# A gated recurrence with a feed-forward layer on one core: the second group's decay steps on VectorE, and all steps in a new order

## The chip, the cores and the metric

The kernel runs on one core of a Trainium2 chip. The metric is the time of one execution on the device in microseconds. Before the change it is 265.83 us, the median of five runs (265.01 to 266.19).

The engines are called as the profile calls them: PE (TensorE) for matmuls, DVE (VectorE) and POOL (GpSimd) for elementwise work, ACT (ScalarE) for functions such as Exp, Ln, Arctan, Sin and Tanh, SP (SyncE), which issues most of the DMAs. POOL issues some DMAs too.

## The reference

Inputs are q, k, v, a_re and a_im, each of shape (4 batches, 8 heads, 768 steps, 48 channels) in float32, and three weights, 384x1536, 384x1536 and 1536x384. A complex recurrence runs over the steps; its real part is read out with q, and the result, seen as 3072 tokens of 384, goes through a gated feed-forward layer.

```
mag = sqrt(a_re*a_re + a_im*a_im)
scale = minimum(mag, 0.999) / (mag + 1e-06)
ar, ai = a_re*scale, a_im*scale
for t in range(S):
    new_re = ar*S_re - ai*S_im          # (ar, ai at step t, along d)
    new_im = ar*S_im + ai*S_re
    S_re, S_im = new_re + outer(k[t], v[t]), new_im
    y[t] = q[t] @ S_re
x = y as (3072, 384)
out = (sigmoid(x @ w_gate) * (x @ w_val)) @ w_out
```

## The kernel before

**Slabs and groups.** The 768 steps are cut into 6 chunks of 128, so there are 24 slabs (chunk c, batch b), numbered m = 4c + b. Slabs are worked on in eight groups g of 2, 2, 4, 4, 4, 4, 2, 2 (SIZES, L34). Group 0 is slabs 0 and 1, group 1 is slabs 2 and 3, all of chunk 0; group 2 is chunk 1, and so on.

**The steps of a group, by the names that the kernel gives them.**
- lr, la: a_re and a_im of a slab into one tile `a` (L556, SP). sq: both squared (L583 on DVE for slabs 2 to 8, else L586 on ACT).
- add: the sum of the two squares (L592). min: the cap, min and max in one instruction for two slabs (L599). lnm: Ln of it (L613, ACT). cl: its sum over the steps of the chunk, a matmul with a triangle (L633). ee: Exp of half of it with both signs (L640, L642). scr, rbe, arr: the chunk's last row through DRAM into columns.
- lna, inv: Ln of a_re, and Exp of minus that, which is 1/a_re (L607, L618, ACT). r: the ratio a_im/a_re for two slabs (L624). atan: its arctangent (L702). hop: the angle at the end of the chunk before, added by a small DMA that POOL issues (L714). ct: the sum of angles over the steps (L722); r16 and nid take whole turns off (L728, L735). cr: the last angle for the next hop (L745). ab, cs: sine and cosine (L756, L767 to L770).
- lk, lq, lv: loads of k, q and v (L556, SP); v16: v as f16 (L688, POOL). qke: k and q times the two decay factors, one instruction for a slab (L695). ks, qs: times cosine and sine, to f16 (L780).
- tp, qkT: transposes on PE and their copy by DVE (L818, L819, L825), from slab 13 on DMA transposes instead. sc: scores (L837). mst: times the causal mask (L845). y: the read-out (L903 with the carried state, L905 with the scores). kv, u, x16, P: the state that is carried from chunk to chunk (L859, L868, L877, L887, L890).
- y16, xp, xt: y to f16, transposed, into the group's input of the feed-forward layer (L522, L923, L929). pg and pv: two times three matmuls for each of 12 blocks of 128 of the 1536 (L942). tanh: the gate on ACT (L952). p: gate times value on DVE (L958). po: the third matmul (L978). ot, st: result to SBUF (L522) and out (L996).

**Which engine.** add, min, r and qke are issued through a helper that takes the group number; with BRISK = 1 (L30) only group 0 has them on DVE:

```
def eng(g):
    return nc.vector if g < BRISK else nc.gpsimd
```

**What sets the order.** The order of all steps is written out by hand, as numbers: TIMES has one number for each step, and the steps are issued in the order of these numbers, each engine getting its instructions in that order and running them in it. A step's waits follow from the data. The numbers serve as sort keys only. Before a function of ACT that the loaded table doesn't have, a table load is put in (L1006).

```
order = sorted(self.steps, key=lambda k: (at[k], self.rank[k]))
```

SLOTS names, tile by tile in order of allocation, which of a kind's few buffers the tile gets (2 buffers for `a2`, `sq`, `lm`, `cs`, 5 for `qk`, 4 PSUM banks each for `gen` and `moe`, and so on). WARM names steps ahead of which PE multiplies a tile of zeros a number of times, into the tile that the step then overwrites (L1012); there are 465 such matmuls in all.

```
for _ in range(WARM.get(key, 0)):
    nc.tensor.matmul(warm_of(tiles[st[2][0]]), zero, zero, start=True, stop=True)
st[0](tiles)
```

The nine weight loads (wg, wv, wo, thirds of w_gate, w_val and w_out, L541 and L548) are issued by POOL between its other instructions, at places that TIMES sets too. The first six feed pg and pv: blocks 0 to 3 need the first third, 4 to 7 the second, 8 to 11 the last.

Of the kernel before, what the change touches and what calls it, by code (L numbers as in the profile page):

```python
# [29 lines left out]
BRISK = 1  # L30
# [6 lines left out]
        32.951, 14.583, 29.638],  # L37
    "wv": [
        41.185, 24.111, 37.481],
    "wo": [  # L40
        56.204, 51.226, 63.509],
    "lr": [
        0.04, 0.86, 3.16, 5.08, 13.925, 19.752, 28.021, 17.531, 29.623,
        62.128, 43.583, 64.048, 57.026, 74.047, 73.257, 65.008, 96.257,
        107.615, 110.045, 101.515, 137.663, 151.768, 166.927, 171.067],
    "la": [
        2.2, 0.45, 4.12, 7, 14.68, 15.64, 25.512, 24.552, 30.593, 69.119,
        51.877, 58.495, 61.138, 75.967, 72.847, 63.088, 97.077, 105.695,
        103.265, 102.675, 139.203, 141.828, 168.878, 168.468],
    "sq": [  # L50
        5.69, 4.73, 9.161, 10.49, 21.424, 23.242, 34.706, 33.84, 44.15,
        72.689, 57.636, 69.729, 66.044, 80.249, 76.577, 70.689, 104.472,
        112.973, 118.73, 115.322, 149.228, 158.967, 174.676, 175.97],
    "add": [
        6.559, 7.025, 10.178, 12.149, 22.441, 26.922, 36.527, 34.857, 53.807,
        73.594, 58.541, 70.634, 66.949, 89.758, 79.981, 72.602, 111.571,
        123.103, 119.884, 117.287, 150.133, 161.218, 175.581, 177.193],
    "min": [
        7.605, 13.68, 30.458, 38.521, 74.873, 71.699, 91.293, 87.116, 124.638,
        121.415, 162.282, 179.123],  # L60
    "lna": [
        6.558, 13.727, 35.687, 78.872, 83.739, 120.761, 160.998, 178.729],
    "lnm": [
        8.185, 15.332, 39.488, 82.363, 93.681, 125.605, 163.249, 180.206],
    "inv": [
        7.426, 14.595, 37.195, 80.986, 91.565, 126.982, 163.986, 180.943],
    "r": [
        8.295, 15.623, 42.005, 39.424, 82.531, 84.291, 93.956, 106.636,
        133.282, 137.885, 164.891, 181.848],
    "cl": [  # L70
        9.073, 9.719, 20.075, 17.308, 43.684, 45.402, 46.048, 42.48, 85.5,
        91.202, 87.197, 87.843, 109.442, 108.149, 111.386, 107.503, 148.529,
        150.473, 145.491, 154.559, 177.162, 179.303, 182.338, 182.984],
    "ee": [
        12.987, 12.247, 22.019, 22.759, 47.25, 48.311, 49.051, 46.51, 90.085,
        92.941, 89.345, 90.825, 111.417, 110.677, 112.233, 109.46, 152.06,
        151.32, 152.8, 155.406, 179.466, 188.022, 187.282, 188.762],
    "scr": [
        30.033, 30.313, 28.711, 28.431, 49.147, 48.867, 50.638, 56.303,
        91.661, 94.511, 90.731, 91.381, 115.548, 116.608, 114.858, 110.455,  # L80
        156.012, 152.178, 156.292, 156.982, 183.077, 198.269, 192.333, 192.613],
    "rbe": [
        47.412, 67.694, 70.599, 98.417, 129.307, 159.322, 213.64, 204.94],
    "lk": [
        9.88, 6.04, 7.96, 20.712, 35.106, 41.425, 53.205, 32.273, 78.847,
        81.727, 83.647, 77.887, 115.138, 96.667, 104.225, 133.664, 114.448,
        116.198, 156.572, 141.418, 176.447, 181.157, 169.288, 172.027],
    "lq": [
        11.8, 10.84, 22.632, 21.672, 38.894, 46.157, 55.893, 37.894, 79.807,
        92.351, 91.941, 82.687, 120.194, 101.105, 109.085, 134.074, 119.784,  # L90
        117.158, 157.262, 146.226, 177.407, 184.327, 178.947, 183.367],
    "lv": [
        23.592, 12.76, 50.228, 49.427, 8.92, 75.007, 80.767, 76.927, 92.761,
        84.607, 114.038, 111.965, 119.374, 136.703, 106.655, 128.527, 145.816,
        94.101, 111.005, 121.814, 191.923, 206.91, 205.76, 172.987],
    "v16": [
        31.509, 17.384, 57.244, 54.761, 13.104, 79.404, 86.539, 81.909,
        103.832, 104.408, 118.728, 120.839, 130.217, 145.197, 110.655,
        132.706, 169.908, 113.392, 127.88, 168.466, 198.411, 218.557, 220.232,
        183.609],  # L100
    "qke": [
        15.915, 14.389, 27.877, 25.162, 49.465, 52.046, 61.748, 47.704,
        95.717, 97.478, 99.239, 92.196, 128.457, 115.039, 135.043, 141.784,
        155.763, 152.242, 166.705, 157.524, 186.109, 196.651, 188.357, 193.916],
    "atan": [
        10.216, 19.618, 43.84, 86.41, 117.353, 147.043, 184.404, 190.796],
    "ct": [
        11.426, 13.076, 25.634, 21, 49.401, 50.047, 52.307, 54.263, 92.496,
        93.142, 95.408, 90.356, 130.362, 122.671, 135.255, 129.716, 155.205,
        163.471, 166.078, 164.117, 193.531, 197.936, 199.73, 198.917],  # L110
    "r16": [
        12.273, 13.923, 26.481, 25.575, 50.248, 50.894, 55.627, 62.519,
        93.343, 96.075, 99.028, 91.869, 133.139, 123.937, 138.869, 133.605,
        156.052, 164.944, 167.011, 169.332, 195.244, 199.482, 202.877, 203.943],
    "nid": [
        13.722, 14.523, 27.081, 26.727, 50.848, 51.817, 56.538, 64.118,
        95.245, 96.701, 104.303, 94.435, 135.093, 128.568, 141.444, 137.196,
        156.948, 165.748, 170.162, 171.619, 196.323, 200.376, 205.919, 214.499],
    "cr": [
        19.248, 20.355, 30.395, 30.765, 55.525, 55.895, 58.653, 66.781,  # L120
        97.782, 101.447, 107.796, 98.152, 137.227, 144.056, 144.426, 141.165,
        158.597, 170.192, 185.618, 173.352],
    "ab": [
        18.25, 15.449, 28.61, 27.546, 52.95, 52.484, 59.067, 64.782, 95.609],
    "cs": [
        18.25, 17.363, 28.61, 29.608, 52.95, 54.738, 59.067, 64.782, 100.183,
        99.026, 106.162, 103.315, 135.456, 129.652, 141.807, 139.532, 157.44,
        166.112, 170.562, 172.195, 196.687, 201.864, 206.282, 214.862],
    "ks": [
        19.692, 18.716, 29.74, 32.974, 54.147, 56.093, 63.916, 66.125,  # L130
        102.751, 101.019, 108.206, 110.129, 136.745, 130.941, 143.096,
        148.631, 159.249, 167.943, 175.372, 184.196, 200.213, 210.119,
        207.571, 216.165],
    "qs": [
        22.29, 20.558, 31.205, 37.37, 57.07, 59.923, 69.298, 68.432, 104.816,
        101.885, 109.263, 110.995, 140.302, 131.807, 145.477, 149.497,
        164.078, 170.962, 176.838, 185.062, 202.011, 215.299, 208.437, 222.773],
    "tp": [
        28.731, 23.29, 26.28, 21.645, 35.6, 35.154, 40.597, 38.934, 62.039,
        59.39, 67.868, 65.458, 81.249, 79.852, 77.107, 78.532, 112.679,  # L140
        117.708, 115.091, 104.466, 123.54, 114.644, 118.804, 116.388, 153.513,
        146.785],
    "qkT": [
        30.606, 24.977, 26.947, 28.012, 36.771, 39.279, 41.245, 39.878,
        62.985, 61.255, 71.71, 74.679, 82.056, 81.125, 77.755, 79.552,
        116.498, 118.355, 115.9, 107.008, 125.003, 115.301, 120.485, 117.097,
        154.826, 147.433],
    "sc": [
        34.93, 31.247, 28.504, 30.801, 37.762, 40.012, 47.846, 43.126, 76.333,
        76.557, 78.978, 75.783, 86.974, 84.274, 80.298, 82.023, 119.651,  # L150
        121.374, 116.834, 113.126, 125.91, 123.317, 125.687, 122.248, 157.111,
        156.075, 151.119, 152.639, 160.33, 155.851, 159.057, 158.834, 180.596,
        180.82, 189.87, 191.616, 191.84, 190.093, 194.8, 194.577, 219.4,
        214.661, 221.347, 220.274, 218.527, 226.605, 227.483, 227.707],
    "mst": [
        35.572, 32.375, 29.076, 36.172, 41.843, 40.476, 48.271, 43.55, 78.953,
        76.981, 80.151, 78.354, 87.398, 85.118, 83.72, 82.654, 121.084,
        122.149, 117.695, 114.102, 126.711, 124.403, 126.111, 123.338,
        157.717, 157.118, 151.561, 153.064, 161.349, 156.518, 160.75, 160.15,
        181.021, 181.62, 190.294, 192.041, 193.106, 190.894, 195.71, 196.309,  # L160
        220.361, 217.63, 222.173, 220.96, 219.761, 227.029, 227.908, 230.424],
    "kv": [
        56.338, 51.617, 68.314, 72.159, 91.002, 102.808, 115.538, 122.471,
        120.524, 138.006, 153.959, 132.303, 168.667, 157.334, 171.782,
        177.808, 201.834, 215.532, 216.379, 220.497],
    "P": [
        58.601, 52.018, 75.994, 73.548, 91.403, 113.636, 119.553, 122.872,
        121.683, 145.011, 154.36, 134.071, 173.896, 158.317, 173.43, 178.209,
        211.584, 218.829, 219.295, 223.639],
    "y": [  # L170
# [238 lines left out]
def kernel(  # L409
# [107 lines left out]
    def eng(g):  # L517
        return nc.vector if g < BRISK else nc.gpsimd

# [523 lines left out]
```

## Time and profile before

| | |
|---|---|
| median of five runs | 265.83 us (265.01 to 266.19) |
| the profiled execution | 265.22 us |
| its span, first to last instruction | 263.5 us |
| busy PE, DVE, ACT, POOL | 95%, 80%, 69%, 62% of the span |
| TensorE clock granted | 1.00 throughout |
| matmuls of zeros (L1012) | 465, 31.9 us busy |
| sums on POOL, L592 | 22, 1302 ns mean; on DVE 2, 554 ns |
| caps on POOL, L599 | 11, 889 ns mean; on DVE 1, 560 ns |
| ratios on POOL, L624 | 11, 1883 ns mean; on DVE 1, 950 ns |
| decay products on POOL, L695 | 22, 2054 ns mean; on DVE 2, 1791 ns |
| bytes moved | 38.18 MB, 145 GB/s mean |

The span begins with the first and ends with the last instruction; the execution's time has some 1.7 us more around it. A mean over a form is the time of one instruction from its start to its end; successive instructions of an engine overlap a little, so the distance of their starts is shorter than that (0.48 us between sums on DVE that take 0.55). On PE the overlap is larger: three matmuls of 128x512 are shown as 0.81 us and start 0.65 us after the three before them.

### The profile page before, as it was taken

The numbers are of one execution on the slowest core, as the hardware profiler recorded it, in microseconds if no ns is written. First come the engines' busy times: TensorE is split into PE (matmuls) and PEld (weight loads), VectorE is DVE, ScalarE is ACT, GpSimd is POOL, SyncE is SP. The second block draws the span as 40 slices with busy tenths as digits, with TensorE's granted clock in tenths as the row PEclk, the third lists the DMA queues.
The fourth block names the chain that finished last, engine by engine and source line by source line (L and its number), as shares of the span: only waits on it lengthen the run. The fifth ranks groups of instructions, "written<-read, shape, count | busy, mean of one in ns | idle before, by whom it ended". The sixth has DMA issues, their size and how long they took to land.

```text
span 263.5 us, 6444 instructions
## 1 busy us (share of the span) xinstructions
PE 250.4 (95%) x2445; PEld 172.9 (66%) x2445; DVE 211.6 (80%) x373; ACT 182.5 (69%) x304; POOL 163.3 (62%) x170
## 2 busy tenths in 40 slices
PE   8797898899899999999999999999999999999995
PEld 8576786668688854547764457754556644678784
DVE  2778798489989965999989888988668978986552
ACT  3999356975468999989586897889993665114250
POOL 1284889799069999759999969782879400420000
PEclk9999999999999999999999999999999999999999
DMA  7999999999988929999729998689986288641001
GB/s 142 214 163 197 191 186 201 154 171 197 175 98 161 217 52 194 156 201 201 146 63 165 208 149 147 92 198 175 200 159 73 91 151 140 63 119 63 30 32 60
DMA packets 175022, 38.18 MB, mean 145 GB/s; under 512 B 167928, under 2 KB 174992, under 8 KB 174992
## 3 DMA queue, kind: packets, MB, share of 16 engines
q1 hardware_dynamic: 170368, 34.20, 68.9%
q0 software_dynamic: 4624, 3.57, 9.8%
q8 instruction: 19, 0.31, 0.5%
q14 instruction: 11, 0.09, 0.1%
HBM read 30.74 MB, written 4.76 MB: 135 GB/s over the span
## 4 chain that ended last, share of the span: by engine, by line
PE 72%; SPq 9%; DVE 7%; ACT 6%; issue 3%; DMA 3%; DVEq 0%; ACTq 0%
PE o L978 18%; PE v L942 16%; PE g L942 15%; SPq L556 9%; PE cl L633 5%; PE ct L722 4%; PE sc L837 4%; PE y L905 2%; PE y L903 2%; PE tp L818 2%; PE tp L819 1%; DVE qst L780 1%; DMA a<-in_a_re_dram 1%; PE xp L923 1%; PE kv L877 1%
## 5 line engine op out<-in xcount | busy, mean ns | idle before, releaser
L952 ACT ACTIVATE g<-g 128x256 f16<-128x256 f32 (+1 forms) x96 | 44.6, 492 | 37.5 <-PE g L942 28.7
L958 DVE SCALAR_TENSOR_TENSOR p<-g,v 128x256 f16<-128x256 f16 (+1 forms) x96 | 50.5, 548 | 14.6 <-PE v L942 7.6
L942 PE MATMUL v<-xt,wv 128*128 128x256 f16 (+1 forms) x288 | 58.4, 326 | 1.3 <-DVE p L958 1.2
L942 PE MATMUL g<-xt,wg 128*128 128x256 f16 (+1 forms) x288 | 58.0, 325 | 0.4 <-DVE p L958 0.3
L978 PE MATMUL o<-wo,p 128*128 128x384 f16 (+1 forms) x300 | 55.6, 319 | 0.0
L592 POOL TENSOR_TENSOR lm<-sq 128x384 f32<-128x384 f32 x22 | 28.6, 1302 | 29.4 <-ACT sq L586 14.6
L695 POOL TENSOR_TENSOR qk<-qk,ee 128x768 f32<-128x768 f32 x22 | 43.6, 2054 | 1.1 <-DMA qk<-in_q_dram 0.8
L942 PEld LDWEIGHTS <-wv 128*128 128x128 f16 x288 | 27.3, 98 | 20.8 <-issue 3.4
L942 PEld LDWEIGHTS <-wg 128*128 128x128 f16 x288 | 27.4, 97 | 19.6 <-issue 3.2
L845 DVE TENSOR_TENSOR mst<-sc,msk_t 128x512 f16<-128x512 f32 x48 | 31.8, 683 | 7.5 <-PE sc L837 6.9
L978 PEld LDWEIGHTS <-p 128*128 128x128 f16 x300 | 27.1, 98 | 13.0 <-issue 0.2
L1006 ACT ACT_TABLE_LOAD x27 | 34.6, 1283 | 0.5
L1012 PEld LDWEIGHTS <-zero 128*128 128x128 f16 x465 | 29.9, 103 | 6.5 <-issue 4.6
L780 DVE TENSOR_TENSOR kst<-qk,cs 128x768 f16<-128x768 f32 x24 | 25.0, 1043 | 2.3 <-ACT cs L770 1.3
L780 DVE TENSOR_TENSOR qst<-qk,cs 128x768 f16<-128x768 f32 x24 | 25.3, 1059 | 0.0
L624 POOL TENSOR_TENSOR a<-a 128x768 f32<-128x768 f32 x11 | 20.7, 1883 | 2.7 <-ACT a L618 2.3
L633 PE MATMUL cl<-lm,wl_t 128*128 128x384 f32 x48 | 19.6, 504 | 2.7 <-ACT lm L613 2.0
L714 POOL DMA_DIRECT2D a<-cr x20 | 16.9, 1030 | 5.9 <-ACT a L702 5.5
L688 POOL TENSOR_SCALAR v<-v 128x384 f16<-128x384 f32 x24 | 16.2, 675 | 5.7 <-DMA v<-in_v_dram 2.9
L722 PE MATMUL ct<-a,wt_t 128*128 128x384 f32 x48 | 19.6, 503 | 0.1
L825 DVE COPY qkT<-tp 128x1024 f16<-128x1024 f16 x26 | 17.4, 682 | 1.3 <-PE tp L819 1.1
L768 ACT ACTIVATE cs<-ct 128x384 f32<-128x384 f32 x24 | 11.8, 491 | 9.4 <-DVE cs L756 9.4
(71 smaller groups left out, 441.2 us busy)
## 6 DMA issues: line engine op xcount, KB each, us to landing
a<-in_a_re_dram SPq DMA_DIRECT2D x24, 192.0 KB
a<-in_a_im_dram SPq DMA_DIRECT2D x24, 192.0 KB
qk<-in_k_dram SPq DMA_DIRECT2D x24, 192.0 KB
v<-in_v_dram SPq DMA_DIRECT2D x24, 192.0 KB
qk<-in_q_dram SPq DMA_DIRECT2D x24, 192.0 KB
out_dram<-ot SPq DMA_DIRECT2D x23, 192.0 KB
wg<-in_moe_w_gate_dram POOLq DMA_DIRECT2D x3, 384.0 KB, 6.0
wv<-in_moe_w_val_dram POOLq DMA_DIRECT2D x3, 384.0 KB, 5.9
```

The lines of the kernel that those rows point to most:

```text
L592: eng(g).tensor_tensor(out=T[LM][:, s], in0=T[SQ][:, 0], in1=T[SQ][:, 1], op=ALU.add)
L633: nc.tensor.matmul(T[CL][:, :HD], wl_t, T[LM][:, s], start=True, stop=True)
L695: eng(g).tensor_tensor(out=T[QK], in0=T[QK], in1=T[EE], op=ALU.mult)
L722: nc.tensor.matmul(T[CT][:, :HD], wt_t, T[A][:, 1, s], start=True, stop=False, skip_group_check=True)
L780: nc.vector.tensor_tensor(out=T[SL][i].rearrange("p h (r x) -> p h r x", r=2)[:, :, :, 0:D], in0=heads(T[QK][:, i]).unsqueeze(2) .broadcas ...
L845: nc.vector.tensor_tensor(out=T[MS], in0=T[SC], in1=msk_t.unsqueeze(1).broadcast_to([L, 4, L]), op=ALU.mult)
L942: nc.tensor.matmul(T[ACC][:, :nt], w[:, j, fb * 128:fb * 128 + 128], T[XT][:, j, :nt], start=(j == 0), stop=(j == 2))
L952: nc.scalar.activation(out=T[G16][:, :nt], in_=T[PG][:, :nt], func=FT.Tanh, scale=0.5)
L958: nc.vector.scalar_tensor_tensor(out=T[PT][:, fb, :nt], in0=T[G16][:, :nt], scalar=1.0, op0=ALU.add, in1=T[PV][:, :nt], op1=ALU.mult)
L978: nc.tensor.matmul(T[PO][:, :wd], T[PT][:, fb, s * L:(s + 1) * L], wo16[:, fb, c0:c0 + wd], start=(fb == 0), stop=(fb == NFB - 1))
L1006: nc.scalar.preload_act_table_set(SETS[key[1]])
L1012: nc.tensor.matmul(warm_of(tiles[st[2][0]]), zero, zero, start=True, stop=True)
```

## The change

BRISK goes from 1 to 2, so that add, min, r and qke of group 1 are issued on DVE. These are two sums (128x384), one cap, one ratio and two decay products (128x768 each). TIMES, SLOTS and WARM have new numbers throughout: every kind of step has other sort keys, most tiles another buffer, and there are 411 matmuls of zeros in other places. No function is changed.

```
-BRISK = 1
+BRISK = 2
...
     "wg": [
-        32.951, 14.583, 29.638],
+        37.288, 33.328, 40.992],
     "wv": [
-        41.185, 24.111, 37.481],
+        14.906, 24.802, 28.527],
...
     "min": [
-        7.605, 13.68, 30.458, 38.521, 74.873, 71.699, 91.293, 87.116, 124.638,
-        121.415, 162.282, 179.123],
+        7.605, 12.962, 27.624, 38.328, 80.098, 69.74, 90.34, 81.001, 123.736,
+        125.795, 162.811, 178.675],
...
     "qke": [
-        15.915, 14.389, 27.877, 25.162, 49.465, 52.046, 61.748, 47.704,
...
+        18.035, 17.169, 29.555, 25.694, 49.066, 51.647, 62.667, 53.408,
...
     "ct": [
-        11.426, 13.076, 25.634, 21, 49.401, 50.047, 52.307, 54.263, 92.496,
...
+        11.649, 13.132, 19.238, 23.515, 49.004, 51.593, 52.239, 53.926,
...
     "hop": [
-        45.384, 45.964, 46.544, 47.124, 88.598, 89.178, 90.713, 88.018, 127.3,
...
+        45.249, 46.049, 47.583, 48.163, 89.76, 88.6, 89.18, 88.02, 128.08,
...
 WARM = {
-    ('cl', 0): 86,
-    ('ct', 0): 19,
-    ('ct', 1): 18,
-    ('sc', 0, 0): 62,
-    ('sc', 0, 1): 4,
-    ('sc', 1, 0): 15,
-    ('sc', 1, 1): 18,
...
-    ('cl', 2): 38,
-    ('cl', 3): 47,
-    ('ct', 2): 34,
-    ('ct', 3): 5,
...
+    ('cl', 0): 78,
+    ('ct', 0): 23,
+    ('ct', 1): 15,
+    ('sc', 0, 0): 21,
+    ('sc', 0, 1): 8,
+    ('sc', 1, 0): 71,
...
+    ('cl', 2): 16,
+    ('cl', 3): 69,
+    ('ct', 3): 19,
+    ('sc', 2, 0): 23,
...
```

How the front of each engine's order changes, as far as it is spoken of below:
- DVE, between the ratio of group 0 and the last square of group 2. Before: sq of slabs 2 and 3, r16 of 0 and 1, qke, ab, qke, ab, ks, ks, qs, sq, qs, sq, a qkT copy, r16 of 3 and 2, and so on. After: sq, add, sq, add of group 1, r16 of slab 0, min, r16 of slab 1, ab, r of group 1, two qke of group 0, ab, ks, ks, qs, qs, sq, r16 of 2 and 3, sq, qke of slab 3, ab, two qkT copies, ab, sq, qke of slab 2, a copy, ks, qs, a mask, ks, sq.
- ACT, after its second table load. Before: four Exp of group 0 (ee), lna, inv, lnm of group 1, table, cs, cs, cr, atan. After: lna, four Exp, lnm, inv, table, cs of slab 1, atan, cs of slab 0.
- POOL. Before, it begins with the two sums of group 1. After: cast of v, first third of w_val, cast of v, a sum of group 2 and so on; the last two sums of group 2 are followed by the first third of w_gate, the cap, a ratio, the last third of w_gate, a ratio, two hops, a sum of group 3, two hops.
- PE: the first of pg and pv is preceded by seven cl, eight tp and five sc in place of eight, eight and seven. Past it there are 88 matmuls of zeros in place of 78.
- SP: the 16th to 27th loads are the same kinds in another order; the stores of slabs 2 and 3 stand later among the loads.

## The prediction

> **What bounds the kernel now.** I read the page's busy times first, then the same by stretch, then the chain that ended last, then each engine's instructions in order of time up to 90 us.
>
> ```profile
> PE 250.4 (95%) x2445; PEld 172.9 (66%) x2445; DVE 211.6 (80%) x373; ACT 182.5 (69%) x304; POOL 163.3 (62%) x170
> ```
> ```profile
> 10.00:48.00 38.00, 32.56 (x439) 26.98 (x439) 31.55 (x45) 28.03 (x38) 27.74 (x23) 1.00 1.09 190
> 48.00:60.00 12.00, 11.64 (x106) 8.32 (x107) 7.43 (x15) 10.17 (x23) 11.81 (x10) 1.00 0.97 160
> 60.00:90.00 30.00, 28.77 (x359) 24.16 (x357) 28.63 (x56) 20.32 (x35) 20.13 (x25) 1.00 0.99 163
> 90.00:240.00 150.00, 149.59 (x1277) 89.59 (x1275) 128.34 (x216) 112.17 (x188) 102.30 (x105) 1.00 0.77 144
> ```
> After the stretch and its length come busy PE, weight load, DVE, ACT and POOL, the granted clock, the DMA share. PE is busy everywhere, but in the front with matmuls of zeros (L1012, 465 of them). DVE is idle 6.45 us of 10 to 48 and 4.57 of 48 to 60, and then busy 28.63 of 30: from 60 to 90 it sets the pace. After 90 it is PE.
>
> How much of PE's time is work follows from the starts of its rows: three 512-wide matmuls of L942 start 0.65 after each other, three 256-wide 0.33, four of L978 0.65, a cumulative sum (L633, L722) 0.65 to 0.70, eight transposes 0.45, four score products 0.22, eight of L905, L903 or L877 0.20, L735 and L923 0.17. Times their counts: 62 + 31.5 (L942), 47 (L978), 31.5 (L633, L722), 11.6, 10.6, 12.8 (y and kv), 8: 215 us. The span is 263.5, so 48.5 is not work. The first L942 starts at 49.54; eight cl, four ct, eight tp, seven sc, four nid, two y and two xp, 14.9 us, stand ahead of it, so 34.6 is lost in the front; 3.1 lies behind PE's end (260.4), and 10.8 between. That 10.8 holds 78 of the zero matmuls at 0.056 each, 4.4 us. So only the front, and the pace of DVE up to 90, have much to give.
>
> ```profile
> 37.51 2.61 POOL L592 TENSOR_TENSOR lm<-sq 128x384 f32<-128x384 f32 x2 [1.15 <-DVE sq L583]
> 43.60 0.83 POOL L541 DMA_DIRECT2D wv<-in_moe_w_val_dram  x1
> ```
> ```profile
> 48.08 1.56 PE L633 MATMUL cl<-lm,wl_t 128*128 128x384 f32 x4 [0.71 <-DVE xt L929]
> 49.54 0.50 PE L942 MATMUL v<-xt,wv 128*128 128x256 f16 x3
> ```
> The columns are start and duration. The front ends with two things at once: xt of group 0, which PE awaits at 48.08, and the first third of w_val, issued by POOL at 43.60 and landing a median 5.9 later, 49.5.
>
> **The change part by part.** *Six instructions of group 1 (slabs 2 and 3).* POOL loses two sums (1.30 mean), a cap (0.89), a ratio (1.88) and two decay products (2.05): 2.6 + 0.9 + 1.9 + 4.1 = 9.5 us. DVE gains them at group 0's rows, start to start: 2 x 0.48, 0.48, 0.87, 2 x 0.95: 4.2 us. POOL was not what ended the front (27.74 of 38), so its 9.5 us alone are worth nothing; what could count is the shorter chain and DVE's 4.2.
>
> ```profile
> 17.23 1.84 POOL L624 TENSOR_TENSOR a<-a 128x768 f32<-128x768 f32 x1
> ```
> ```profile
> 15.92 1.02 DVE L695 TENSOR_TENSOR qk<-qk,ee 128x768 f32<-128x768 f32 x1
> 17.33 2.57 DVE L695 TENSOR_TENSOR qk<-qk,ee 128x768 f32<-128x768 f32 x1
> ```
> The same product took 1.02 alone and 2.57 beside POOL's ratio, which ended at 19.07: it stood still until then and then took its 0.8. That POOL ratio is one of the moved steps, so 1.55 us of DVE stall leaves the front with it: DVE's net is +2.65 there.
>
> [...]
>
> *The front, in the new order.* From before's times: DVE squares slab 2 at 10.24 as before, sums and squares slab 3, done 13.0; r16 of slab 0 waits for ct until 14.0; the cap is done by 15.0. ACT loads its table at 13.79, takes Ln of a, four Exp of group 0, Ln of the cap at 16.2, Exp at 17.0 to 17.9. Here the change adds a wait: DVE's ratio stands at 17.0 for ACT's Exp until 17.9, with group 0's two products and ks queued behind it; ks starts at 21.0, not 20.3. Arctan of group 1 starts at 20.0, not 21.71, and both ct of group 1 are done at 25, not 28.8. DVE then has seventeen instructions without a hole, 12.4 us by their rows, up to the last square of group 2: 37.1, before 38.3. POOL's two sums end at 39.7 (2.61), the issue of w_gate's first third at 40.6, the cap at 41.4; Ln at 42.9 (before 43.26). PE then goes cl of slab 5, y, two more cl, xp: xt at 46.0 instead of 48.3. The weight that is needed first is now issued at 39.7 and lands at 45.7; it was 49.5. First L942: 46.1, 3.4 earlier. But one cl and two sc (1.1 us) are now behind it, so PE's loss in the front falls by 2.3.
>
> *What DVE owes then.* I summed DVE's instructions in both orders up to marks. Up to group 0's xt the new order holds 0.9 us more: 4.2 added, 3.3 put off (three masks, a qkT copy, a square). Up to group 1's xt it is 5.6 more, and 4.2 to 4.7 at nearly every later mark. So past xt DVE has 3.3 us more to do, starting 2.3 earlier. If it idles as before (4.57 + 1.37 up to 90) it is 1.0 late at 90; if it fills the holes, all 2.3 stays. The largest hole, 2.66 us, is a mask waiting for a score product behind L942; the next, 1.29, waits for ct of group 2, which hangs on Arctan and the hops (POOL's small DMAs). By the same steps Arctan of group 2 comes at 45.8 instead of 46.31, and the hops are now split in two pairs by a sum of 1.3 us, so the last two come no earlier. I take the 0.5 that Arctan moves: -0.5, ends -2.3 and +1.0.
>
> *Zero matmuls.* 411 in place of 465; those missing are in the front, where they fill waits: nothing. Past the first L942 there are 88 in place of 78: +0.6 by 0.056 each.
>
> *The rest of the order.* Every PE, DVE, ACT, POOL and SP instruction past 90 us has another neighbour, and PSUM and SBUF slots rotate differently; stores of slabs 2 and 3 go out after the next groups' loads on SP. No row of before shows those waits. The bound below: of the 6.4 us lost there without zeros, a gain of 1.0. Above: the stretch where the chain left PE for ACT, 94.6 to 102.5, repeated at a worse place; it holds 7.9 us of ACT time and cost PE only about 0.3; at half cover gone, 3.5. I take +0.8, nearer to the covered row: PE has 149.59 of 150 busy there, so an order can lose more than it can win.
>
> **Sum:** -0.5 + 0.6 + 0.8 = +0.9 on a span of 263.5, 264.4. The profiled execution took 265.22 around its span; the median of five runs is 265.83. Put on that: 266.7.
>
> **Rivals.** *The front's gain is kept* (faster): place, 48 to 60 us; it decides if DVE fills at least 3.3 of its 4.57 idle there. For it: POOL has 9.5 us less to do, and xt and the weight both come earlier. Against it: group 2's chain moves only 0.5. Price -2.3 + 0.6 - 0.4: 263.7. *A wait in the new order of the dense stage* (slower): one engine held by an in-order neighbour, as ACT's Exp and Ln of two groups do at 97 to 100.5, but where PE has no other product in front. Price 3: 268.8. For it: DVE carries 4.2 more all the way to 90, with 1.4 idle. Against: after 100 us PE's named waits total under 1 us. *The move itself does nothing* (POOL is off the path, gain and new waits cancel): 265.8.
>
> **How the numbers follow.** Forecast 0.40, front kept 0.30, dense wait 0.22, nothing 0.08. Under 0.3% (0.8 us) a measurement can't be told from no change. The forecast's own spread of 1.2 puts about 0.25 above +0.8, 0.11 inside, 0.04 below. With the other cases: faster 0.04 + 0.30 = 0.34, same 0.11 + 0.08 = 0.19, slower 0.25 + 0.22 = 0.47. The ends of the terms add to -2.7 and +5.1, 263.1 to 270.9; since the extremes need all terms at once I take 263.2 to 269.6. The forecast's own range is 265.5 to 267.9.
>
> **What would show it.** Right: DVE's product of group 0 near 1.0 with no 2.57; a DVE wait for ACT's Exp ahead of the ratio near 17 us; first L942 near 46; DVE again over 95% busy from 60 to 90; group 2's first L942 no earlier than before. Wrong: first L942 at 48 or later (then a load or PE's 71 zeros ahead of a score product hold the front), or DVE with holes from 60 to 90 and PE's dense stage starting 2 us earlier (front kept), or a PE wait over 1 us after 100 (dense wait).

## The result and the profile after

The kernel after takes 268.99 us, the median of 36 executions (264.99 to 271.98); on the same chips the kernel before took 266.19, the median of 71 (264.72 to 267.63). The ratio is 1.0044, with a 95% interval of 1.0026 to 1.0062: slower, with the lower end of the interval just under the 0.3% that can be told from no change. That ratio leaves out executions more than 1.5% above the fastest of their kernel, here 19 of the 36, so that means over all executions are given beside it below: 268.62 against 266.17, +2.45.

The profiled execution took 266.51, with a span of 264.8 (before 265.22 and 263.5). Its busy times, from the page:

```profile
span 264.8 us, 6328 instructions
...
PE 248.4 (94%) x2391; PEld 171.5 (65%) x2391; DVE 217.3 (82%) x379; ACT 182.0 (69%) x303; POOL 155.2 (59%) x164
```

DVE has six instructions more and POOL six fewer, as the change says. DVE is busy for 5.7 us more. The moved instructions account for 4.2 and the old stall of 1.55 is gone, so some 3 us of new stalls must be in there. The busy time by stretch (columns as before: PE, weight load, DVE, ACT, POOL, granted clock, DMA share, GB/s):

```profile
10.00:48.00 38.00, 31.74 (x385) 25.83 (x386) 33.55 (x48) 28.82 (x40) 16.56 (x17) 0.96 1.08 190
48.00:60.00 12.00, 11.29 (x119) 8.52 (x117) 9.01 (x19) 8.20 (x17) 11.13 (x10) 1.00 1.03 157
60.00:90.00 30.00, 27.36 (x335) 22.91 (x335) 27.79 (x49) 20.09 (x38) 21.43 (x24) 1.00 1.02 174
90.00:240.00 150.00, 149.08 (x1286) 89.56 (x1283) 130.47 (x217) 112.67 (x187) 104.85 (x105) 1.00 0.77 141
```

Up to 60 us DVE fills more of its time than before (33.55 and 9.01 in place of 31.55 and 7.43). From 60 to 90, PE has lost 1.41 (27.36, before 28.77), and that is where the kernel falls behind. The granted clock in the front is 0.96, before 1.00. In order of time (start, duration, engine, line, idle time ahead of it), the front:

```profile
17.74 1.28 DVE L628 TENSOR_TENSOR a<-a 128x768 f32<-128x768 f32 x1 [0.63 <-ACT a L622]
18.94 1.81 DVE L699 TENSOR_TENSOR qk<-qk,ee 128x768 f32<-128x768 f32 x2
...
46.58 0.36 DVE L933 COPY xt<-xp 128x384 f16<-128x384 f16 x1 [1.28 <-PE xp L927]
```
```profile
46.99 0.22 PE L822 MATMUL tp<-idn_t,kst 128*128 128x128 f16 x1 [0.23 <-DVE xt L933]
...
47.44 0.49 PE L946 MATMUL g<-xt,wg 128*128 128x256 f16 x3
```

The two products of group 0 follow each other without the old 2.57, and the ratio waits 0.63 for ACT. xt of group 0 is complete at 46.94 (before 48.29), and the first feed-forward matmul starts at 47.44 (before 49.54). By group 1 that lead is gone. Before, the two copies were

```profile
47.68 0.61 DVE L929 COPY xt<-xp 128x384 f16<-128x384 f16 x2
...
72.61 0.62 DVE L929 COPY xt<-xp 128x384 f16<-128x384 f16 x2
```

and now:

```profile
65.14 2.98 DVE L784 TENSOR_TENSOR kst<-qk,cs 128x768 f16<-128x768 f32 x1 [0.23 <-issue]
...
72.18 2.78 DVE L784 TENSOR_TENSOR qst<-qk,cs 128x768 f16<-128x768 f32 x2
74.89 0.61 DVE L933 COPY xt<-xp 128x384 f16<-128x384 f16 x2
```
```profile
65.47 1.83 POOL L699 TENSOR_TENSOR qk<-qk,ee 128x768 f32<-128x768 f32 x1
```
```profile
66.55 0.49 PE L946 MATMUL g<-xt,wg 128*128 128x256 f16 x3
68.50 0.44 PE L1016 MATMUL v<-zero 128*128 128x128 f16 x5 [1.46 <-DVE p L962]
```

A kst of group 2 takes 2.98 in place of 0.95, beside a decay product on POOL of the same group, which runs from 65.47 to 67.30; DVE ends at 68.12. A `p` stands behind kst on DVE, and PE waits 1.46 for it. xt of group 1 is copied at 74.89, before at 72.61: 2.3 late, after a lead of 1.35 at group 0. At the end of the span 1.3 of it is left.

### The profile page after: what moved, and what is told of

It reads as the page before. It is cut to its first block, busy times and chain, and to the rows that moved or that the text cites. A ratio compares the mean times of both kernels' runs of the same rounds, so it can differ in the third digit from the quotient of the medians.

```text
span 264.8 us, 6328 instructions
## 1 busy us (share of the span) xinstructions
PE 248.4 (94%) x2391; PEld 171.5 (65%) x2391; DVE 217.3 (82%) x379; ACT 182.0 (69%) x303; POOL 155.2 (59%) x164
## 4 chain that ended last, share of the span: by engine, by line
PE 70%; ACT 10%; DVE 9%; issue 4%; DMA 4%; SPq 0%; POOL 0%; ACTq 0%; DVEq 0%
PE o L982 16%; PE g L946 15%; PE v L946 15%; PE ct L726 5%; PE cl L637 4%; PE sc L841 3%; DMA qk<-in_k_dram 3%; ACT L1010 2%; DVE kst L784 2%; PE tp L822 2%; ACT lm L617 1%; PE y L909 1%; PE y L907 1%; DMA a<-in_a_re_dram 1%; PE xp L927 1%
## 5 line engine op out<-in xcount | busy, mean ns | idle before, releaser
L946 PE MATMUL v<-xt,wv 128*128 128x256 f16 (+1 forms) x288 | 59.0, 325 | 0.1
L982 PE MATMUL o<-wo,p 128*128 128x384 f16 (+1 forms) x300 | 55.0, 319 | 0.2
L699 POOL TENSOR_TENSOR qk<-qk,ee 128x768 f32<-128x768 f32 x20 | 38.7, 1961 | 6.5 <-DVE qst L784 2.8
L596 POOL TENSOR_TENSOR lm<-sq 128x384 f32<-128x384 f32 x20 | 23.6, 1182 | 20.8 <-DVE sq L587 10.8
L1016 PEld LDWEIGHTS <-zero 128*128 128x128 f16 x411 | 28.1, 107 | 8.0 <-issue 5.9
L784 DVE TENSOR_TENSOR kst<-qk,cs 128x768 f16<-128x768 f32 x24 | 26.9, 1124 | 0.8 <-ACT cs L774 0.5
L784 DVE TENSOR_TENSOR qst<-qk,cs 128x768 f16<-128x768 f32 x24 | 26.0, 1090 | 0.0
L628 POOL TENSOR_TENSOR a<-a 128x768 f32<-128x768 f32 x10 | 18.0, 1814 | 3.4 <-ACT a L622 3.2
L590 ACT ACTIVATE sq<-a 128x768 f32<-128x768 f32 x17 | 14.3, 854 | 6.2 <-DMA a<-in_a_re_dram 5.0
```

Source lines behind the costliest of these rows:

```text
L596: eng(g).tensor_tensor(out=T[LM][:, s], in0=T[SQ][:, 0], in1=T[SQ][:, 1], op=ALU.add)
L699: eng(g).tensor_tensor(out=T[QK], in0=T[QK], in1=T[EE], op=ALU.mult)
L784: nc.vector.tensor_tensor(out=T[SL][i].rearrange("p h (r x) -> p h r x", r=2)[:, :, :, 0:D], in0=heads(T[QK][:, i]).unsqueeze(2) .broadcas ...
L946: nc.tensor.matmul(T[ACC][:, :nt], w[:, j, fb * 128:fb * 128 + 128], T[XT][:, j, :nt], start=(j == 0), stop=(j == 2))
L982: nc.tensor.matmul(T[PO][:, :wd], T[PT][:, fb, s * L:(s + 1) * L], wo16[:, fb, c0:c0 + wd], start=(fb == 0), stop=(fb == NFB - 1))
```

## The experiments

Times stand against the kernel before on the same chip; its mean was 265.87 (29 executions) for the first four, 265.78 (35) for the next four, 265.59 (23) for the next two and 265.80 (23) for the last two. "Difference" is between the means over all executions; the ratio is taken as above. The standard error of a mean is 0.13 to 0.52, that of a kernel before 0.09 to 0.17.

| run | median | range | n | above 268 | difference | ratio, 95% interval |
|---|---|---|---|---|---|---|
| after | 268.99 | 264.99 to 271.98 | 36 | 24 | +2.45 | 1.0044 [1.0026, 1.0062] |
| e1_engine_only | 267.40 | 266.29 to 268.34 | 12 | 1 | +1.36 | 1.0053 [1.0034, 1.0072] |
| e2_order_only | 269.84 | 268.67 to 270.19 | 5 | 5 | +3.65 | 1.0133 [1.0105, 1.0161] |
| e3_no_late_zeros | 268.32 | 264.62 to 270.19 | 12 | 6 | +2.07 | 1.0020 [0.9992, 1.0048] |
| e4_front_filled | 267.85 | 265.50 to 269.73 | 12 | 5 | +1.61 | 1.0044 [1.0013, 1.0074] |
| e5_first_gap | 266.33 | 264.40 to 269.71 | 12 | 4 | +1.20 | 1.0027 [0.9997, 1.0056] |
| e6_all_gaps | 266.59 | 265.42 to 270.17 | 12 | 2 | +1.07 | 1.0026 [1.0002, 1.0049] |
| e7_before_first_gap | 265.77 | 264.64 to 266.32 | 12 | 0 | -0.05 | 0.9997 [0.9975, 1.0018] |
| e8_gaps_product_later | 265.23 | 263.78 to 266.08 | 12 | 0 | -0.64 | 0.9977 [0.9955, 1.0000] |
| e9_product_only | 266.03 | 264.84 to 268.56 | 12 | 2 | +0.86 | 1.0036 [1.0007, 1.0065] |
| e10_first_gap_product | 264.75 | 263.35 to 265.99 | 12 | 0 | -0.87 | 0.9962 [0.9939, 0.9985] |
| e11_repaired_on_pool | 267.48 | 266.16 to 268.79 | 12 | 1 | +1.66 | 1.0068 [1.0045, 1.0090] |
| e12_before_product | 266.43 | 265.54 to 267.52 | 12 | 0 | +0.64 | 1.0018 [0.9995, 1.0042] |

### The two halves of the change alone

The engine move in the old order (the kernel before with one edit):

```
-BRISK = 1
+BRISK = 2
```

> The kernel before, its order kept, with the six steps of group 1 on VectorE alone (BRISK 2). Theory (the loss is the new order between 47 and 75 us, not the engines): DVE gains 4.2 us of work in an order that left POOL room for it, and loses the 1.55 us stall of the decay product beside POOL's ratio; first FFN matmul within 0.5 us of 49.5; time within 0.7 us of before. Rival (DVE's added work is what costs): the 4.2 us come out at the end in part, 1 to 3 us slower, with DVE still over 95% busy from 60 to 90 us.

267.40, slower by 0.5%: the theory's "within 0.7" was wrong, the rival's size was right, though DVE is busy for 28.28 of the 30 us from 60 to 90, 94% and not over 95%. DVE's order of time shows how the move is paid for:

```profile
27.61 0.96 DVE L695 TENSOR_TENSOR qk<-qk,ee 128x768 f32<-128x768 f32 x1 [0.58 <-DMA qk<-in_q_dram]
...
31.20 0.96 DVE L695 TENSOR_TENSOR qk<-qk,ee 128x768 f32<-128x768 f32 x1 [0.64 <-DMA qk<-in_q_dram]
```

Moved to DVE, each product takes 0.96, but in the old order it stands there ahead of its q load, and DVE waits 0.58 and 0.64 with all that is queued behind. xt of group 0 was copied at 49.37 in place of 47.68. PE waits another 1.1 for a third of w_val, so the feed-forward layer starts some 2.9 late (the first mask behind its first matmuls at 53.89 in place of 50.95), and xt of group 1 is still 2.4 late (75.02).

The new order with the six instructions on POOL (the kernel after with `BRISK = 1`):

> The changed kernel's order with the six steps back on POOL (BRISK 1). Theory: POOL's sums, cap, ratio and products (9.5 us) now stand in front of DVE's r16, masks and copies in an order not made for them, so the front is late by 2 to 5 us and the whole 2 to 5 us slower than the changed kernel. Rival (the engines are beside the point, the order alone makes the difference): within 0.7 us of the changed kernel, that is 0.5 to 2.5 us slower than before.

All five executions lie at 268.67 or above. The last xt copy of group 0 is 2.8 later than in after (49.34 and 46.58), as the theory said of the front; the whole is 0.9 slower than after between the medians and 1.2 between the differences, which lies between the theory's 2 to 5 and the rival's 0.7. Two things stand out in its trace. First the front, by stretch and in order of time:

```profile
12.00:14.00 2.00, 2.00 (x13) 1.32 (x12) 1.27 (x1) 1.97 (x3) 1.11 (x2) 0.50 1.07 212
```
```profile
1.04 6.04 PE L1016 MATMUL cl<-zero 128*128 128x128 f16 x78 [1.04 <-DVE zero L496]
...
10.56 2.47 PE L637 MATMUL cl<-lm,wl_t 128*128 128x384 f32 x4 [3.49 <-ACT lm L617]
12.83 2.24 PE L1016 MATMUL ct<-zero 128*128 128x128 f16 x23
```

The 78 zero matmuls ahead of the first cumulative sum lasted 6.04 us (7.13 in the profile of after), so that PE then stood idle for 3.49 us (2.29 there):

```profile
1.04 7.13 PE L1016 MATMUL cl<-zero 128*128 128x128 f16 x78 [1.04 <-DVE zero L496]
10.46 1.56 PE L637 MATMUL cl<-lm,wl_t 128*128 128x384 f32 x4 [2.29 <-ACT lm L617]
```

Behind the gap of 3.49 the granted clock is 0.50: the sum takes 2.47 in place of 1.56, the 23 zeros 2.24 in place of 1.45. Second, the same collision of kst and product as in after: 2.98 at 68.45.

### Zeros late and zeros early

Without the 88 zero matmuls past the first feed-forward matmul (14 entries of WARM deleted):

```
-    ('pg', 0, 3): 4,
-    ('pv', 0, 5): 10,
...
```

> The changed kernel without the 88 matmuls of zeros past the first FFN matmul. Theory (they are on PE's path, 0.056 us each, 4.9 us busy, but most fill waits for DVE): 0.3 to 1.5 us faster than the changed kernel, clock 1.0 past 46 us. Rival (they keep the clock up): the granted clock falls below 1.0 somewhere between 46 and 90 us and the time is the same or longer.

Mean 0.4 under that of after against its own before (+2.07 and +2.45), with a standard error near 0.6: their cost, estimated at 0.6, can't be confirmed or excluded. The runs spread from 264.62 to 270.19, so late zeros are not what makes after spread. The clock is 1.00 from 46 us on in its trace, as the theory said. That trace is of a late execution, 269.03; up to the first feed-forward matmul its order is that of after, and it is read below.

58 zero matmuls more, into a PSUM bank that nothing reads, ahead of later steps of the front. In the trace of after PE stands idle for 1.10 us ahead of 28.90 and 0.85 ahead of 30.36, and the granted clock is 0.50 from 30.5 to 33.5 us (0.94 and 0.65 in the half microseconds around it):

```
+FILL = {('cl', 2): 16, ('ct', 3): 8, ('tp', 0, 1): 18, ('tp', 0, 0): 16}
...
+            for _ in range(FILL.get(key, 0)):
+                nc.tensor.matmul(spare[:, :L], zero, zero, start=True, stop=True)
```

> The changed kernel with 58 more matmuls of zeros into a spare bank where PE idles between 21 and 30.4 us (before cl of slab 2, ct of slab 3, and two transposes of slab 0). Theory (PE's idle time there lets the granted clock fall to about half for 3.4 us, and this is why the changed kernel's times scatter over 265 to 272): clock 1.0 in the front in the profile, scatter of the runs down to about that of before (2 to 3 us wide), median 0.5 to 2 us faster than the changed kernel. Rival (the clock's fall lies under DVE's work and the scatter is from elsewhere): clock 1.0 but scatter and median as before the edit.

Five executions at 265.50 to 266.55 and seven at 267.75 to 269.73: two groups, and no cure. The mean granted clock of each execution is on record: 1.000 in the five, 0.986 to 0.994 in the seven. The gap ahead of the first cumulative sum is still there: in its trace, which is of one of the five, the cumulative sums wait 3.3 us in all for ACT's Ln, in that of after 3.0, of which that gap is 2.29.

That gap alone (2.29 in the trace of after, 3.34 in that of e3, where the clock is 0.78, 0.50 and 0.86 in the three stretches of 2 us from 10 to 16), closed:

```
-    ('cl', 0): 78,
+    ('cl', 0): 114,
```

> The changed kernel with 114 in place of 78 matmuls of zeros ahead of the first cl, so that PE is busy until about 9 to 10.3 us in place of 7.1 to 8.2. Theory (PE's idle stretch there reaches 3.4 us in some executions, the granted clock then falls to half from 11.4 to 15 us, ct of slab 0 comes 1.6 us late and the front with it): the upper half of the changed kernel's times goes, median 0.8 to 2 us below that of the changed kernel, few runs over 268.5. Rival (the scatter comes from the loads or from the later gaps at 28 to 36 us): the median within 0.5 us of the changed kernel, times still up to 270.

Median 266.33 in place of 268.99, but four executions are still above 268. Its profiled execution (264.40) shows the collision with the other outcome:

```profile
64.70 0.96 DVE L784 TENSOR_TENSOR kst<-qk,cs 128x768 f16<-128x768 f32 x1 [0.23 <-issue]
```
```profile
65.04 2.29 POOL L699 TENSOR_TENSOR qk<-qk,ee 128x768 f32<-128x768 f32 x1
```

Here kst takes its 0.96 and the product on POOL is the longer one (2.29, in after 1.83); xt of group 1 comes at 72.40. The stagger of the starts is the same as in after (0.34 and 0.33), so it doesn't tell which of the two is held up.

Both fillings together (114, and 72 zeros in the spare bank at 21 to 36 us):

> The changed kernel with PE's idle stretches of the whole front filled: 114 zeros ahead of the first cl, and 72 into a spare bank between 21 and 36 us. Theory (with the clock whole the changed order is worth what before is worth: the fast five of the run with the later gaps filled lay at 265.5 to 266.5): times within 265 to 267.5, median within 0.6 us of before, clock 1.0. Rival (the new order itself is 1 us slower, as forecast): median 0.8 to 1.5 us above before with clock 1.0.

266.59, mean +1.07 beside e5's +1.20: once the first gap is closed, closing the later ones brings nothing that can be told. The median is 0.80 above before, where the rival begins, but the profiled execution, 270.17, is far outside the theory's range though the first gap is closed in it (0.54). It and the late execution of the run without late zeros have one thing in common, DVE idle ahead of the same square of group 2:

```profile
33.38 0.96 DVE L588 TENSOR_TENSOR sq<-a 128x768 f32<-128x768 f32 x1 [2.06 <-issue]
```
```profile
33.94 0.96 DVE L573 TENSOR_TENSOR sq<-a 128x768 f32<-128x768 f32 x1 [1.76 <-issue]
```

The first line is of e6, the second of e3; in after that square starts at 31.28 with no idle time ahead of it. The last xt copy of group 0 comes at 49.73 and 50.32, in after at 46.58. What the square waited for the profile doesn't name; a load of `a` that lands late would fit and is not shown. In e6 the clock is 1.00 up to 36 us, so this delay doesn't need a fall of the clock.

The same closing in the kernel before (`('cl', 0): 86` to `116`):

> The kernel before with 116 in place of 86 matmuls of zeros ahead of the first cl. Theory (before never reaches the clock's fall in that gap, its 86 zeros leave at most 2.9 us idle): same as before within 0.3%. Rival (part of before's own spread of 264.7 to 267.6 is the same fall): spread down to under 2 us and median 0.3 to 1 us lower.

-0.05 us: nothing to gain there (the range is 1.7 us wide, as the rival said, but the median is not lower). In the profile of before, the gap is 1.96 us and the clock 1.00 throughout; the theory's 2.9 is an estimate, 86 zeros at the pace of e2 (78 in 6.04) ahead of a sum at 10.56. So more zeros are not a gain of their own; in the new order they repair a loss.

### The collision taken out

e6 with one sort key changed, so that POOL's product of slab 6 comes behind a cast of v:

```
-        18.035, 17.169, 29.555, 25.694, 49.066, 51.647, 62.667, 53.408,
+        18.035, 17.169, 29.555, 25.694, 49.066, 51.647, 64.5, 53.408,
```

> The run with all gaps of the front filled, and the decay product of slab 6 on POOL moved behind the cast of v of slab 2, so that it no longer runs beside the k product of 65 us (2.98 us there in place of 0.95). Theory (DVE sets the pace from 60 to 90 us, so a stall of 2.0 us there is paid): 0.8 to 2 us faster than the run with all gaps filled, group 1's xt earlier by as much. Rival (the stall is hidden or another two-input product meets POOL instead): within 0.4 us of it.

265.23, no execution above 266.08, 1.71 less in the mean than e6 and 1.36 less in the median: the theory's 0.8 to 2. To see whether the two causes are separate, the same key alone, and the key with the first gap closed:

> One sort key of the kernel after: POOL's decay product of slab 6 comes behind the cast of v of slab 2 (62.667 becomes 64.5); all zero matmuls are as in the kernel after. Theory of two separate costs (the clock's fall behind PE's gap ahead of the first cumulative sum, and the collision of kst with POOL's product at 65 us): kst lasts 0.95 in place of 2.98, xt of group 1 is copied at 72.4 to 73 in an execution with a whole clock, the fastest runs are near 264, but 3 or more of 12 runs still lie above 268, since the gap is left as it is; median 265.5 to 267.5. Rival, the collision alone makes the spread (an execution is late because it lost it): at most one run of 12 above 267, median near 265.3. Rival, the clock alone counts: as the kernel after, median 267.5 to 269.

> The kernel after with 114 zero matmuls ahead of the first cumulative sum in place of 78 and POOL's decay product of slab 6 behind the cast of v of slab 2; no zeros in a spare bank. Theory: both costs are gone, 265.2 +- 0.4 median, at most one run of 12 above 267, 0 to 0.4% under the kernel before. Rival, the 72 zeros at 21 to 36 us were needed too (later idle stretches of PE bring the clock down by themselves): 3 or more of 12 runs above 267.5, median 265.5 to 266.5.

With after and e5 these make a square. The differences of the means from before:

| | product in place | product moved |
|---|---|---|
| 78 zeros ahead of the first sum | +2.45 (after) | +0.86 (e9) |
| 114 zeros | +1.20 (e5) | -0.87 (e10) |

The product's place is worth 1.6 and 2.1, the zeros 1.2 and 1.7: in the means the two costs add, within their errors of about 0.5. By the ratios of the table the product is worth 0.2 and 1.7, the zeros 0.5 and 2.0: there each mend shows in full only when the other is made too. e9's median lies in the interval of the theory of two costs (two executions above 268, not the three it asked for), outside those of both rivals; in its trace kst takes 0.96 and xt of group 1 is copied at 72.88, as said. e10 was expected at 265.2 and gives 264.75; the rival that the later zeros were needed falls. e10 is the fastest kernel of the study, 0.38% under before (0.15 to 0.61%). Its stretches:

```profile
10.00:48.00 38.00, 30.96 (x389) 24.73 (x390) 33.66 (x49) 29.07 (x41) 17.24 (x18) 1.00 1.08 190
48.00:60.00 12.00, 11.23 (x117) 8.40 (x115) 8.96 (x19) 8.17 (x17) 10.86 (x10) 1.00 1.04 183
60.00:90.00 30.00, 28.20 (x346) 23.44 (x345) 27.33 (x51) 21.20 (x38) 22.62 (x25) 1.00 1.04 179
```
```profile
64.67 0.96 DVE L784 TENSOR_TENSOR kst<-qk,cs 128x768 f16<-128x768 f32 x1 [0.23 <-issue]
...
70.48 2.77 DVE L784 TENSOR_TENSOR qst<-qk,cs 128x768 f16<-128x768 f32 x2
73.18 0.61 DVE L933 COPY xt<-xp 128x384 f16<-128x384 f16 x2
```

The clock is whole in the front, and from 60 to 90 PE has won back 0.84 of its 1.41. The two qst still take 2.77 beside POOL's sums (71.34 to 74.11), in place of 1.82 for two at 23.07 in after, so xt of group 1 is 0.6 later than before and not earlier.

### What the engine move is worth when the order fits it

e10 with the six instructions back on POOL (`BRISK = 1`):

> The new order with 114 zero matmuls ahead of the first cumulative sum and POOL's decay product of slab 6 moved (264.75 with BRISK = 2), but BRISK = 1: the six instructions of group 1 are back on POOL, nothing else differs. Theory: in this order the move to DVE is worth something, since on POOL the two sums, the cap, the ratio and the two products take 9.5 in place of 4.2 in the chain to Arctan of group 1 and in front of POOL's sums of group 2; last xt copy of group 0 at 47.5 to 49 in place of 46.1, median 266.3 to 267.8 with a clock of 0.99 to 1.0. Rival, the move is worth nothing and the order alone made e2_order_only slow through the clock: xt within 0.5 of 46.1, median 264.4 to 265.3.

267.48 and xt of group 0 at 48.68: as the theory said. In this order the move to DVE is worth 2.7 us between the medians (264.75), 2.5 between the differences from before. e11's front, beside that of e2, also shows the clock without the gap (0.69 us of idle PE in place of 3.49):

```profile
12.00:14.00 2.00, 2.00 (x29) 1.64 (x27) 1.10 (x2) 1.97 (x3) 0.93 (x2) 1.00 1.02 201
```
```profile
10.27 1.56 PE L637 MATMUL cl<-lm,wl_t 128*128 128x384 f32 x4 [0.69 <-ACT lm L617]
11.67 1.45 PE L1016 MATMUL ct<-zero 128*128 128x128 f16 x23
```

29 matmuls run in the stretch in which e2 has 13, and the first r16 starts at 13.85, in e2 at 15.81. Of these 1.96 us, 0.66 are left at xt of group 0 (49.34 and 48.68), and with the collision 2.87 at xt of group 1 (78.19 and 75.32): 2.0 of stall, and about what was left of the front's delay. So a fall of the clock behind the first gap, for all that it holds up the first r16, costs some 0.7 us by these two traces, less than the 1.2 and 1.7 that the zeros are worth in the mean.

Last, a collision that the kernel before has itself, and which its trace shows

```profile
63.36 2.20 DVE L780 TENSOR_TENSOR qst<-qk,cs 128x768 f16<-128x768 f32 x1
```
```profile
62.93 1.82 POOL L695 TENSOR_TENSOR qk<-qk,ee 128x768 f32<-128x768 f32 x1
```

with POOL's product put behind a weight load:

```
-        15.915, 14.389, 27.877, 25.162, 49.465, 52.046, 61.748, 47.704,
+        15.915, 14.389, 27.877, 25.162, 49.465, 52.046, 63.6, 47.704,
```

> The kernel before with one sort key changed: POOL's decay product of slab 6 (62.93 to 64.75 in its trace, beside qst, which took 2.20 in place of 0.95) comes behind the issue of the last third of w_out. Theory, a collision of this kind is paid whole when it lies ahead of an xt copy that DVE's order sets: qst lasts 0.95, xt of group 1 is copied 0.8 to 1.3 earlier than 72.61, median 264.6 to 265.2; then most of what the new order has over the kernel before (264.75) can be had without it. Rival, the kernel before has its cover there (PE or ACT sets xt of group 1): xt at 72.3 to 72.7, median 265.5 to 266.0.

A miss: the edit did not take the collision away. DVE ran later too, and the two met again, worse:

```profile
64.01 2.74 DVE L780 TENSOR_TENSOR qst<-qk,cs 128x768 f16<-128x768 f32 x1
```
```profile
64.10 1.83 POOL L695 TENSOR_TENSOR qk<-qk,ee 128x768 f32<-128x768 f32 x1
```

xt of group 1 is copied at 73.81, 1.2 later than before. So whether before would gain from a dodge was not tried, and stays open.

## Why the prediction was right, and where it was not

The forecast was 266.7 and slower; the ratio puts the kernel after at 267.0 on the 265.83 of before. By the means over all executions it is 268.3, beyond the forecast's own 265.5 to 267.9 and inside the whole range of 263.2 to 269.6. Three of the five signs that it named came: the product, the wait, and group 2 no earlier (its first xt copy at 94.17, before at 90.56). In the profiled execution two terms missed and cancelled, so that 266.7 lies so near is in part luck; a third, set at nothing, makes the mean over all executions larger.

**The front (-2.3): right in direction, too large.** The ratio's wait for ACT near 17 us (17.74, 0.63 idle) and the product without 2.57 came as said; Arctan of group 1 starts at 19.82 (20.0), the weight load is issued at 40.08 (39.7). But the last square of group 2 runs from 37.13 to 38.07, where 37.1 was said for its end (before 38.28): the seventeen instructions without a hole had one of 0.64, a wait for ct. xt is complete at 46.94, not 46.0, and the sum had put the first feed-forward matmul right behind xt, while eight transposes (0.45) and a wait of 0.23 stand between. It starts 2.1 earlier, not 3.4; less the 1.1 of work that is now behind it, the front gives 1.0.

**What DVE owes (net -0.5): the step that failed.** xt of group 1 comes 2.3 later. From the end of group 0's xt to the start of group 1's DVE takes 27.95 us, before 24.32: 3.6 more, where the step had 1.8 (3.3 of work, less 1.5 of holes filled). The holes came nearly as said: DVE is idle for 3.55 there, before 4.96. But it is busy for 24.40 in place of 19.36. Of these 5.0 some 1.0 is stall: kst and qst run 3.0 over their 0.95 in after (2.03 of it the kst), and 2.0 in before. The other 4.0 is work; the step had 3.3, though by its own marks 5.6 less 0.9, 4.7, was due by this point. The 0.5 that the step let Arctan of group 2 move did not come either: it starts at 46.47 (said 45.8, before 46.31).

To the stalls past the front the prediction gave no price: it looked for collisions only in the front, where the moved instructions stand (the 1.55 beside POOL's ratio). The collision that decided is 40 us later, between two instructions that were not moved; the new order put them side by side. Without it (e10) the same stretch takes 26.76, 2.4 more than before, nearer to the step's 1.8.

**Zeros (+0.6 late, nothing in the front): the second half failed.** "Those missing are in the front, where they fill waits: nothing" is wrong for those ahead of the first sum: 36 more there win 1.2 to 1.7 us in the mean (the square). That the eight which the new order took away, 86 to 78, would have been enough was not tried. The way from the zeros to the time is shown in part. Behind gaps of 3.34 (e3) and 3.49 (e2) the clock was 0.50 from 12 to 14 us, behind gaps of 2.29 (after) and 2.33 (e9) it was 1.00. The mean clock of each execution of after goes with its time: the 16 at 0.981 to 0.987 have a mean of 269.5, the 20 at 0.992 to 1.000 one of 267.9. But no late execution of after itself was traced, and the trace of e3, with the same front, has more than the fall in it: its first r16 is 1.6 late, of which 0.6 is left at the first square of group 2 (25.40 and 24.80), and then comes the wait of 1.76. The 0.6 for the late zeros stays unproved (e3).

**The rest of the order (+0.8): not borne out.** From xt of group 1, 2.3 late, to the end, 1.3 late, the new order wins 1.0, zeros included, where the two terms said +1.4. By the prediction's own marks DVE has 5.6 more up to xt of group 1 and 4.2 to 4.7 later, so a part of that 1.0, or all of it, may be DVE's and not the order's. This and the failed DVE term (2.8 too low) cancelled to a sum of +0.9 against a measured +1.3 on the span.

**The rivals.** No dense-stage wait: past 100 us PE's named waits sum to 0.2 us. "The front's gain is kept" asked that DVE fill 3.3 of its 4.57 idle from 48 to 60; it filled 1.6 (9.01 busy, before 7.43), and not even e10, at 264.75, has the lead left at xt of group 1. DVE did not stay over 95% busy from 60 to 90 (27.79 of 30, 93%): its stall shows as a longer instruction (kst, 2.98), and behind it PE waits 1.46 for DVE's `p` and DVE 0.33 for PE.

**What stays open.** Four of the six executions of after with a mean clock of 1.00 took 267.95 to 269.32, more than a stall of 2.03 on top of the fastest (264.99) explains. No trace was taken of one of them. With the product moved and the gap closed (e8 and e10) none of 24 is above 266.08. The wait ahead of a square of group 2 in e3 and e6 is a third delay, which no experiment here touched: what causes it is open, and so is how much of what the square of four kernels gives to the zeros and the product is owed to its coming or not.

## What to carry to other kernels

An order tuned as a whole is to be repaired at its collisions before the engine choice in it is judged: here the same six instructions on VectorE cost 0.5% in the old order and won about 1% in the repaired one. After any reordering, look down the trace for instructions of VectorE and GpSimd that overlap and last longer than alone, wherever they stand: here a product on VectorE took 2.98 us in place of 0.95 beside one of 1.83 on GpSimd, and neither had been moved to another engine. Matmuls that only keep PE busy are to be counted against the length of the gap that they leave at their fastest (78 of them left 2.29 to 3.49 us, and 36 more were worth 1.2 to 1.7 in the mean), not by whether PE had time for them.

## What the hardware showed that was not expected

**The clock falls on some executions of one kernel.** The 78 zeros start at 1.04 in the traces of after, e3 and e2; they last 7.13 us in after, 6.07 in e3 and 6.04 in e2. The faster they run there, the longer the gap behind them (2.29, 3.34 and 3.49): after gaps of 0.46 (e10), 0.69 (e11), 1.96 (before), 2.29 and 2.33 us (e9) the granted clock stays 1.00 from 12 to 14 us, after 3.34 and 3.49 it is 0.50. The length of the last gap alone doesn't set it: the fall in after at 30.5 us stands behind gaps of 1.10 and 0.85. What brings the clock down is not shown by these runs. The fall in e9 at 30 to 34 us, where its clock is 0.51 and 0.64 and that of e10 1.00, cost little: xt of group 0 is copied at 46.18 and 46.06.

**Which of two colliding instructions waits is not told by the recorded starts.** DVE's recorded start is ahead of POOL's by 0.33 in after, 0.35 in e4, 0.34 in e5 and 0.09 in e12; DVE's instruction was the long one in after, e4 and e12 (2.98, 3.00, 2.74) and took its 0.96 in e5. Where it was the long one, it ended 0.82 after POOL's end in all three cases, and alone it takes 0.95: by this estimate most of its work came after POOL's whole instruction.
